# Where the sums over a batch's exponentials stand in the Vector engine's queue, and when the last chunk's exponentials are taken

## The chip, the cores and the metric

The kernel runs on one core of one Trainium2 chip. The time is the device time of one execution in microseconds; a kernel's time is the median of several runs. The kernel before takes 269.26 us (three runs, 268.95 to 269.48).

## The reference

An efficient attention is followed by a layer norm and a two-layer perceptron, for 8 batches of 576 rows, 8 heads of 64 columns (512 columns in all):

```python
q_s = np.exp(q - max(q))                      # over the 64 columns of a head
q_s = q_s / (np.sum(q_s, axis=-1, keepdims=True) + 1e-09)
k_s = exp(k - max(k)) / sum over the rows
kv  = np.einsum('bhsd,bhse->bhde', k_s, v)
x   = np.einsum('bhsd,bhde->bhse', q_s, kv)   # heads side by side: 576 x 512 per batch
xn  = (x - mean) / np.sqrt(var + 1e-06) * g_ln
out = x + np.maximum(xn @ w_ch1, 0.0) @ w_ch2 # 512 -> 2048 -> 512
```

What matters here is the first two lines: for every row and head the exponentials of q are summed, and the reciprocal of the sum scales that head's attention output. The kernel multiplies with the unscaled exponentials first and scales the product afterwards, so the sums are not needed until an attention output is read out of PSUM.

## The kernel before, in words

**Chunks.** A chunk is 512 rows, held as 4 tiles of 128 rows. Chunk c from 0 to 7 is the first 512 rows of batch c; the ninth chunk, `C9` = 8, is the last 64 rows of all eight batches. The chunks' perceptrons run one after the other on TensorE (PE), and everything else is laid beside them: while the perceptron of chunk c runs, the attention of chunk c+1 is computed, and batch c+2 is loaded and its exponentials are taken.

**Stages and positions.** From chunk 2 on the perceptron is written with seven products in place of eight per 2x2 block, and each layer is 112 steps of half a position: the first layer (the first stage, `mm1_fast`, L747) goes from position 0 to 56, the second (the second stage, `mm2_fast`, L677) from 56 to 112. One step is one matmul of 128x128 weights and 256 columns. The order of all engines' instructions is written out by hand: `run` (L830) walks through the matmuls of a chunk and, ahead of each, issues the side work whose position has been reached. Side work at equal positions keeps the order in which it was put on the list. Each engine then works through its own queue in that order and waits there for whatever its next instruction needs.

```python
for weight, go in main:
    while done < len(side) and side[done][0] <= at:
        side[done][1]()
```

**The first stage.** It handles column groups in two halves, groups 0 and 1, then 2 and 3. Each half has seven products with two groups each (`plan`, L788), so each product is 2 positions per group:

```python
(1, "x", True, seed), (5, "b", True, copy_5), (6, "x", False, add_5),
(2, "c", False, relu), (7, "x", False, out_22), (3, "b", False, relu), (4, "x", False, relu)
```

`x`, `b` and `c` are PSUM banks. After product 6 VectorE (DVE) adds `x` and a copy into `b` (`add_5`, L775); product 7 writes on into the same bank `x`, so its first matmul waits until `add_5` of its group has read it. After product 7 DVE makes an output (`out_22`, L778), and after the second group of a half it applies the ReLU to four blocks at once (L783). ScalarE (ACT) makes the copies (L768, L772) and the other ReLUs (L786). `sum_h` (L583) makes the operand sums of the second stage on DVE.

**The second stage.** Products 1, 5, 6, 2, 7, 3 and 4 take 8 positions each. The results are added to the residual by `y_quarter` (L610, eight per chunk), on DVE; the last two read bank `a` after the last product. The PSUM pool has six banks for all of this; the first matmuls on bank `b` of the next chunk wait until `y_quarter` has read the banks that they are put in.

**Attention beside it.** `exp_q` (L193, ACT) writes a batch's exponentials into the tile `eq`, of which there is one buffer; `eq_T` transposes it by a DMA of the SyncE (SP) queue. `reduce_q` (L210, DVE) sums half of the tile over the 64 columns of each head (128x16 sums out of 128x1024 values), twice per chunk, and `recip_q` (L859) takes the reciprocals. `po_mm` multiplies with the key-value product, and `x_fast` (L421, L407, DVE) reads the attention output, scales it by the reciprocals and writes the layer norm's input `xn`. `xn_T` (two DMA transposes on SP, L256) makes `xnT`, and `sum_x` (L248) makes the operand sums `tq` of the next chunk's first stage on GpSimd (POOL); for chunk 7 the second of the four is made on DVE, from the first. `load_batch` writes one element of each input tile on DVE (L1079) ahead of the loads, which SP issues after that.

**The last chunk.** Its rows of q are loaded in chunk 6 (`load_qrem`); `exp_qrem` (L206) takes their exponentials in four pieces on ACT.

Of the kernel before, what the change touches and what calls it, by code (L numbers as in the profile page):

```python
# [20 lines left out]
def kernel(  # L21
# [22 lines left out]
    T = 4  # L44
# [805 lines left out]
    def prep_fast(b):  # L850

        s = [(57, lambda: exp_q(b, 0, 4)), (65, lambda: exp_q(b, 2, 4)), (79, lambda: eq_T(b))]
        s += [(81, lambda: reduce_q(b, 0, 2)), (91, lambda: reduce_q(b, 2, 2))]
        s += [(81, lambda: exp_k(b, 0, 4)), (98, lambda: exp_k(b, 2, 4))]
        s += [(106, lambda: prep_kvrem(b))]
        return s

    def recip_q(c):
        nc.vector.reciprocal(eqs[c][2], eqs[c][1])  # L859

    def attn_fast(c):

        s = [(8, lambda: reduce_q(3, 2, 2))] if c == 3 else []
        s += [(22 if c == 3 else 2, lambda: recip_q(c))]
        s += [(12, lambda: kv_all(c))]
        s += [(40, lambda: start_x(c))]
        for t, (p0, p1) in enumerate(((48, 53), (57, 59), (65, 67), (73, 75))):
            s += spread([lambda t=t, i=i: po_mm(c, t, i) for i in range(NP)], p0, p1)
            s += [(p1, lambda t=t: x_fast(c, t)), ((66, 74, 87, 91)[t], lambda t=t: square_sum(c, t))]
        s += [(61, lambda: xn_T(c, 0, 2)), (78, lambda: xn_T(c, 2, 2)), (95, lambda: rstd_op(c))]  # L870
        s += [((84, 100 if c == C9 - 1 else 88, 92, 101)[i], lambda i=i: sum_x(c, i)) for i in range(4)]
        return s

    def second_side():

        s = [(p, lambda i=i: quarter_w2(i, 1)) for i, p in enumerate((8.5, 13, 44, 46))]
        s += [(8.0, lambda: xn_pT(1, 3, nc.vector))]
        s += [(3, lambda: exp_q(2, 0, 4)), (7, lambda: exp_q(2, 2, 4)), (7.2, lambda: eq_T(2))]
        s += [(42, lambda: square_sum(1, 2)), (67, lambda: square_sum(1, 3)), (71, lambda: rstd_op(1))]
        s += [(7.3, lambda: load_batch(3, (2,), eqTs[2][0:1, T - 1, NP - 1, 0:4])), (31, lambda: load_batch(3, (0,)))]  # L880
        s += [(9 + 2 * j, lambda j=j: cast_v(2, j)) for j in range(2)]
        s += [(7.4, lambda: load_v(3))]
        s += [(93 + j, lambda j=j: cast_v(3, j)) for j in range(2)]
        s += [(15 + 3 * t, lambda t=t: reduce_q(2, t, 2)) for t in (0, 2)]
        s += [(36, lambda: recip_q(2))]
        s += [(18, lambda: exp_k(2, 0, 4)), (22, lambda: exp_k(2, 2, 4)), (26, lambda: prep_kvrem(2))]
        s += [(41, lambda: kv_all(2))]
        s += [(46, lambda: start_x(2))]
        for t, (p0, p1) in enumerate(((52, 54), (57, 59), (62, 65), (70, 74))):
            s += spread([lambda t=t, i=i: po_mm(2, t, i) for i in range(NP)], p0, p1)  # L890
            s += [(p1, lambda t=t: x_fast(2, t)), ((73, 82, 88, 94)[t], lambda t=t: square_sum(2, t))]
        s += [(60, lambda: xn_T(2, 0, 2)), (77, lambda: xn_T(2, 2, 2)), (100, lambda: rstd_op(2))]
        s += [(75, lambda: exp_q(3, 0, 4)), (79, lambda: exp_q(3, 2, 4)), (85, lambda: eq_T(3))]
        s += [(97, lambda: reduce_q(3, 0, 2))]
        s += [(97, lambda: exp_k(3, 0, 4)), (108, lambda: exp_k(3, 2, 4)), (113, lambda: prep_kvrem(3))]
        s += [(p, lambda i=i: sum_w1(i, 1)) for i, p in enumerate((30, 47, 58, 64))]
        s += spread([lambda i=i: sum_x(2, i) for i in range(4)], 95, 108)
        return s

    def attn_rest():  # L900

        s = [(2, lambda: recip_q(C9)), (4, lambda: start_x(C9))]
        for t, (p0, p1, p2) in enumerate(((14, 22, 46), (44, 54, 62), (58, 66, 69), (67, 75, 77))):
            s += [(p0, lambda t=t: [po_mm(C9, t, i) for i in range(NP)])]
            s += [(p1, lambda t=t: x_fast(C9, t)), (p2, lambda t=t: square_sum(C9, t))]
        s += [(61, lambda: xn_T(C9, 0, 2)), (78, lambda: xn_T(C9, 2, 2)), (88, lambda: rstd_op(C9))]
        return s + spread([lambda i=i: sum_x(C9, i) for i in range(4)], 102, 104)
# [179 lines left out]
    with tc.manual_schedule(  # L1087
        engines={mybir.EngineType.PE, mybir.EngineType.DVE, mybir.EngineType.Activation,
                 mybir.EngineType.SP, mybir.EngineType.Pool}
    ):  # L1090
        first_batch()
        load_behind(1, (2, 0))
        load_w2(2)
        load_behind(1, (1,))
        load_w2(3)
        load_behind(2)

        def po_x(c, t):
            for i in range(NP):
                po_mm(c, t, i)  # L1100
            x_fast(c, t)

        run(
            mlp_steps(0),
            [
                (0.5, lambda: xn_pT(0, 1, nc.scalar)),
                (2.5, lambda: (q0_rest(2), x_fast(0, 2))),
                (3.2, lambda: eq_pT(0, 3, nc.scalar)),
                (7, lambda: (q0_rest(3), x_fast(0, 3))),
                (11, lambda: xn_pT(0, 2, nc.scalar)),  # L1110
                (15, lambda: xn_pT(0, 3, nc.scalar)),
                (20, g_columns),
                (24, lambda: square_sum(0, 2)),
                (28, lambda: square_sum(0, 3)),
                (34, lambda: (x_copy(0, 0), square_po(0, 1))),
                (36, lambda: x_copy(0, 1)),
                (37, lambda: nc.vector.tensor_scalar_mul(out=xs[0][3][:, 0, 1:2], in0=xs[0][3][:, 0, 1:2], scalar1=float(DM))),
                (38, lambda: rstd_op(0)),
            ]
            + [(62, lambda: exp_q(1, 0, 4)), (64, lambda: exp_q(1, 2, 4))]  # L1120
            + [(67 + t, lambda t=t: reduce_q(1, t)) for t in range(T)]
            + [((74, 78, 86, 90)[t], lambda t=t: eq_pT(1, t, nc.scalar)) for t in range(T)]
            + [(78, lambda: nc.vector.reciprocal(eqs[1][2], eqs[1][1]))]
            + [(80, lambda: exp_k(1, 0, 4)), (84, lambda: exp_k(1, 2, 4))]
            + [(26 + 4 * i, lambda i=i: scale_w1(i % KO1, i // KO1)) for i in range(2 * KO1)]
            + [(p, lambda i=i: quarter_w2(i, 0)) for i, p in enumerate((55, 58, 60, 62))]
            + [(98.5 + 0.4 * j, lambda j=j: cast_v(1, j)) for j in range(2)]
            + [(p, lambda i=i: sum_w1(i, 0)) for i, p in enumerate((80, 84, 88, 92))]
            + [(100.4, lambda: prep_kvrem(1))]
            + [(100.5, lambda: kv_mm(1, range(T))), (102.0, lambda: (kv_mm(1, range(T, T + 1)), kv_out(1), start_x(1)))]  # L1130
            + [(108.0, lambda: po_x(1, 0)), (110.0, lambda: po_x(1, 1))]
            + [(113.0, lambda: po_x(1, 2)), (114.9, lambda: xn_pT(1, 0, nc.scalar)), (115.9, lambda: square_sum(1, 0))]
            + [(115.9, lambda: po_x(1, 3)), (121.0, lambda: xn_pT(1, 1, nc.scalar)), (122.0, lambda: square_sum(1, 1))]
            + [(128.0, lambda: xn_pT(1, 2, nc.scalar))]

        )
        for c in range(1, B):
            side = []
            if c == 1:
                side += second_side()  # L1140
            else:
                if c + 1 < B:
                    side += attn_fast(c + 1)
                else:
                    side += attn_rest()
                if c + 2 < B:
                    side += [(1, lambda b=c + 2: load_batch(b))]
                    side += [(26, lambda b=c + 2: load_v(b))]
                    side += prep_fast(c + 2)
            if c == B - 2:  # L1150
                side += [(1, load_qrem)]
                side += spread([lambda r=r: exp_qrem(r) for r in range(T)], 34, 50)
                side += [(52, lambda: eq_T(C9))]
                side += [(84 + 4 * t, lambda t=t: reduce_q(C9, t, 2)) for t in (0, 2)]
            sums = [(57, 0)] if c == FAST else [(p, i) for i, p in enumerate((30, 41) if c == B - 1 else (30, 33, 41))]
            run(mlp_steps(c), side + [(at, lambda i=i: sum_h(0, i)) for at, i in sums])
        run(mlp_steps(C9), [(33 + 3 * i, lambda i=i: sum_h(0, i)) for i in range(2)])
# [30 lines left out]
```

## Time and profile before

| | us |
|---|---|
| median of three runs | 269.26 (268.95 to 269.48) |
| profiled execution | 268.44 |
| its span, first to last instruction | 266.6 |
| PE busy | 259.1 (97%) |
| DVE busy | 220.2 (83%) |
| ACT busy | 178.6 (67%) |
| POOL busy | 90.6 (34%) |

The profiled execution is 0.8 us under the median of the runs; 1.8 us of it lie outside the span. Chunk boundaries can be read from the first matmul of a chunk (line L744, `bx<-xnT,w1g`): chunks 2 to 8 begin at 78.77, 105.31, 131.52, 157.73, 183.94, 210.44 and 237.69 us of the span, and the last matmul ends at 262.33. A position of these chunks is 0.218 us (16 matmuls in 1.75 us are 8 positions). Rows of the page and of the timeline give: engine, line, operation, output <- inputs, shape; in brackets the engine's idle time before it and what ended it.

### The profile page before, as it was taken

The page shows a single profiled execution, that of the slowest core. Times are in us where ns is not written, and L with a number is a line of the kernel's source. Part 1 is how long each engine was busy: PE and PEld are TensorE (multiplying, and loading weights), DVE is VectorE, ACT ScalarE, POOL GpSimd, SP SyncE. Part 2 cuts the span into 40 slices and gives each one's busy share as a digit, 9 for nine tenths or more (in the row PEclk, how much of TensorE's full clock was granted, in tenths as well). Part 3 has the DMA queues.
Part 4 walks back from the last instruction along what each step waited for, and adds up shares of the span by engine and source line. Part 5 has one row for each costly group of instructions (what it writes and reads, how often), then busy time and mean ns, then how long its engine had stood idle before and what let it go on. Part 6 is the DMA issues. An engine that isn't in the chain of part 4 may idle for free. (4 is left out here: it accounts for less than half of the span.)

```text
span 266.6 us, 6696 instructions
## 1 busy us (share of the span) xinstructions
PE 259.1 (97%) x2634; PEld 218.4 (82%) x2634; DVE 220.2 (83%) x471; ACT 178.6 (67%) x349; POOL 90.6 (34%) x145
## 2 busy tenths in 40 slices
PE   8999999999999999999999999999999999999993
PEld 5778855775988998899889988998989788888882
DVE  7974995878999899789988988998799968877872
ACT  4767881796966886688668866786686378438400
POOL 6933126213069104930781088109100800030000
PEclk9999999999999999999999999999999999999999
DMA  6999999979966998899589948996935130422014
GB/s 216 220 203 207 325 223 303 278 171 279 176 131 195 303 111 133 246 288 117 92 265 267 127 87 278 257 138 126 261 60 101 42 119 4 79 81 79 2 39 118
DMA packets 82329, 45.00 MB, mean 169 GB/s; under 512 B 58037, under 2 KB 78521, under 8 KB 82298
## 3 DMA queue, kind: packets, MB, share of 16 engines
q0 software_dynamic: 32800, 22.29, 44.9%
q1 hardware_dynamic: 48906, 21.77, 37.6%
q10 hardware_dynamic: 592, 0.52, 0.6%
q8 instruction: 20, 0.33, 0.5%
q14 instruction: 11, 0.09, 0.1%
HBM read 36.70 MB, written 9.44 MB: 173 GB/s over the span
## 5 line engine op out<-in xcount | busy, mean ns | idle before, releaser
L599 PEld LDWEIGHTS <-hs 128*128 128x128 bf16 x512 | 49.5, 98 | 5.7
L744 PEld LDWEIGHTS <-w_q 128*128 128x128 bf16 x448 | 43.0, 98 | 6.8 <-issue 1.0
L248 POOL TENSOR_TENSOR tq<-xnT 128x256 bf16<-128x256 bf16 x24 | 15.6, 665 | 77.2 <-DMA xnT<-xn 63.9
L599 PEld LDWEIGHTS <-hT 128*128 128x128 bf16 x384 | 37.1, 98 | 4.4
L744 PEld LDWEIGHTS <-w1g 128*128 128x128 bf16 x336 | 32.2, 98 | 3.9
L599 PE MATMUL ba<-w_q,hs 128*128 128x256 bf16 x256 | 31.7, 273 | 0.0
L775 DVE TENSOR_TENSOR bb<-bx,s 128x512 f32<-128x512 f32 x28 | 18.3, 695 | 14.1 <-ACT s L772 14.0
L744 PE MATMUL bx<-tq,w_q 128*128 128x256 bf16 x224 | 29.2, 273 | 0.1
L768 ACT COPY bc<-bx 128x512 f32<-128x512 f32 x28 | 15.2, 594 | 16.8 <-PE bx L744 16.8
L421 DVE SCALAR_TENSOR_TENSOR x<-po,rq 128x512 bf16<-128x512 f32 x34 | 23.3, 686 | 2.2 <-PE po L370 2.0
L395 ACT ACTIVATE scrap<-x,mv 128x512 bf16<-128x512 bf16 x32 | 23.0, 720 | 1.7 <-DVE x L421 1.3
L616 POOL DMA_DIRECT2D out_dram<-ot x28 | 15.4, 558 | 24.1 <-DVE ot L610 24.0
L786 ACT ACTIVATE hT<-bc 128x512 bf16<-128x512 f32 x28 | 15.5, 598 | 11.7 <-PE bc L744 11.7
L583 DVE TENSOR_TENSOR hs<-hT 128x1024 bf16<-128x1024 bf16 x32 | 21.7, 685 | 1.3 <-ACT hT L786 1.2
L370 PE MATMUL po<-kv_sb,eqT 128*128 128x128 bf16 x128 | 21.2, 219 | 0.0
L210 DVE TENSOR_REDUCE zq<-eq 128x16 f32<-128x1024 bf16 (+1 forms) x20 | 20.6, 1048 | 0.5 <-ACT eq L193 0.5
L778 DVE TENSOR_TENSOR hT<-bx,s 128x512 bf16<-128x512 f32 x28 | 18.0, 686 | 3.2 <-PE bx L744 3.2
L786 ACT ACTIVATE hT<-bb 128x512 bf16<-128x512 f32 x28 | 15.3, 600 | 8.1 <-PE bb L744 8.1
L624 ACT COPY s<-ba 128x512 f32<-128x512 f32 x15 | 8.7, 579 | 13.4 <-PE ba L599 8.7
L599 PE MATMUL ba<-w_sb,hT 128*128 128x256 bf16 x128 | 16.7, 273 | 0.0
L599 PE MATMUL bb<-w_q,hs 128*128 128x256 bf16 x128 | 16.6, 273 | 0.0
L772 ACT COPY s<-bb 128x512 f32<-128x512 f32 x28 | 15.8, 620 | 0.7 <-PE bb L744 0.7
(152 smaller groups left out, 555.1 us busy)
## 6 DMA issues: line engine op xcount, KB each, us to landing
out_dram<-ot POOLq DMA_DIRECT2D x32, 256.0 KB, 6.2
qt<-in_q_dram SPq DMA_DIRECT2D x5, 1024.0 KB, 6.8
kt<-in_k_dram SPq DMA_DIRECT2D x5, 1024.0 KB, 13.4
w_sb<-in_moe_w_ch_dram POOLq DMA_DIRECT2D x4, 512.0 KB, 16.5
qt<-in_q_dram POOLq DMA_DIRECT2D x2, 1024.0 KB, 14.6
kt<-in_k_dram POOLq DMA_DIRECT2D x2, 1024.0 KB, 15.2
vm<-in_v_dram POOLq DMA_DIRECT2D x16, 128.0 KB, 13.0
w_raw<-in_moe_w_ch_dram POOLq DMA_DIRECT2D x3, 512.0 KB, 12.3
```

The lines of the kernel that those rows point to most:

```text
L210: nc.vector.reduce_sum(eqs[c][1][:, ts], eqs[c][0][:, ts], axis=AX.X)
L248: eng.tensor_tensor(out=dst[:, t], in0=x[:, t], in1=y[:, t], op=ALU.subtract)
L370: nc.tensor.matmul(pobox["p"][:, i * P : i * P + P], eqTs[c][:, t, i, :], kv_sb[:, c, i, :], start=True, stop=True,)
L395: nc.scalar.activation(scrap, x[:, t], AF.Square, bias=mv[:, t, 0:1], scale=-float(DM), accum_out=mv[:, t, 1:2],)
L421: nc.vector.scalar_tensor_tensor(x[:, t].rearrange("p (h d) -> p h d", h=H), in0=pobox[c, t].rearrange("p (h d) -> p h d", h=H), scalar=1. ...
L583: nc.vector.tensor_tensor(out=dst, in0=x, in1=y, op=op)
L599: nc.tensor.matmul(hbox[bank][:, t], lhsT, rhs, start=first and (own or t == 0) and k == 0, stop=k == KH - 1, skip_group_check=True)
L744: nc.tensor.matmul(dst[:, q], lhsT, rhs, start=first and q == 0 and ko == 0, stop=ko == 1, skip_group_check=True)
L772: nc.scalar.copy(at[g, "s"], at[g, "b"])
L775: nc.vector.tensor_tensor(out=at[g, "b"], in0=at[g, "x"], in1=at[g, "s"], op=ALU.add)
L778: nc.vector.tensor_tensor(out=h_out(g, 1, 1), in0=at[g, "x"], in1=at[g, "s"], op=ALU.add)
L786: nc.scalar.activation(h_out(g, odd, half), at[g, name], AF.Relu)
```

## The change

Three things are moved; no instruction is added or taken away, and no shape is changed.

- The two sums of a batch (`reduce_q`) leave the second stage of the chunk in which its exponentials are taken (positions 81 and 91; for batch 3, position 97 of chunk 1 and position 8 of chunk 2) and go into the first stage of the next chunk, to positions 1 and 27. The reciprocal goes from position 2 (batch 3: 22) to 28.
- The same for the ninth chunk: its sums go from positions 84 and 88 of chunk 6 to 1 and 27 of chunk 7, the reciprocal from 2 to 28, and the first `x_fast` of it from 22 to 31.
- In chunk 6 the ninth chunk's exponentials go from positions 34 to 50 (first stage) to 58 to 80 (second stage), and their transpose from 52 to 84.

```diff
     def prep_fast(b):
         s = [(57, lambda: exp_q(b, 0, 4)), (65, lambda: exp_q(b, 2, 4)), (79, lambda: eq_T(b))]
-        s += [(81, lambda: reduce_q(b, 0, 2)), (91, lambda: reduce_q(b, 2, 2))]
         s += [(81, lambda: exp_k(b, 0, 4)), (98, lambda: exp_k(b, 2, 4))]
...
     def attn_fast(c):
-        s = [(8, lambda: reduce_q(3, 2, 2))] if c == 3 else []
-        s += [(22 if c == 3 else 2, lambda: recip_q(c))]
+        s = [(1, lambda: reduce_q(c, 0, 2)), (27, lambda: reduce_q(c, 2, 2)), (28, lambda: recip_q(c))]
         s += [(12, lambda: kv_all(c))]
...
     def second_side():
-        s += [(97, lambda: reduce_q(3, 0, 2))]
...
     def attn_rest():
-        s = [(2, lambda: recip_q(C9)), (4, lambda: start_x(C9))]
-        for t, (p0, p1, p2) in enumerate(((14, 22, 46), (44, 54, 62), (58, 66, 69), (67, 75, 77))):
+        s = [(1, lambda: reduce_q(C9, 0, 2)), (27, lambda: reduce_q(C9, 2, 2)), (28, lambda: recip_q(C9)), (4, lambda: start_x(C9))]
+        for t, (p0, p1, p2) in enumerate(((14, 31, 46), (44, 54, 62), (58, 66, 69), (67, 75, 77))):
...
             if c == B - 2:
                 side += [(1, load_qrem)]
-                side += spread([lambda r=r: exp_qrem(r) for r in range(T)], 34, 50)
-                side += [(52, lambda: eq_T(C9))]
-                side += [(84 + 4 * t, lambda t=t: reduce_q(C9, t, 2)) for t in (0, 2)]
+                side += spread([lambda r=r: exp_qrem(r) for r in range(T)], 58, 80)
+                side += [(84, lambda: eq_T(C9))]
```

On DVE the order around the moved instructions becomes: last `y_quarter`, first sum, `load_batch`'s two writes, `add_5` of groups 0 and 1; and in the middle of the first stage: ReLU (L783), second sum, reciprocal, the two `sum_h`, `add_5` of groups 2 and 3. PE's and POOL's queues keep their order. On SP the ninth chunk's transpose goes behind chunk 7's two `xn_T`.

## The prediction

> **What bounds the kernel now.** First the waits of PE, then the busy time chunk by chunk, then the timelines around what was left.
>
> ```profile
> PE bb L744 <- DVE ot L610: 0.7, 2, 0.5
> PE bb L744 <- DVE kt L1079: 0.2, 1, 0.2
> ```
>
> ```profile
> 78.77:105.31 26.54, 26.37 (x282) 23.34 (x280) 24.54 (x52) 19.72 (x38) 10.66 (x17) 1.00 1.15 187
> 131.52:157.73 26.21, 26.21 (x282) 23.45 (x280) 22.87 (x49) 19.63 (x38) 11.79 (x18) 1.00 1.03 189
> ...
> 183.94:210.44 26.50, 26.37 (x282) 23.43 (x280) 22.92 (x46) 17.49 (x37) 6.59 (x12) 1.00 0.51 119
> 210.44:237.69 27.25, 26.59 (x258) 22.51 (x256) 22.32 (x53) 15.69 (x33) 3.68 (x7) 1.00 0.21 60
> ```
>
> The columns are the chunk's length, then busy PE, weight load, DVE, ACT, POOL, the granted clock, and DMA. Chunks 3, 4 and 5 take 26.21 us each with PE busy throughout: nothing is left to gain there, however much DVE is relieved. Chunk 2 is 0.33 us longer and chunk 6 0.29; chunk 7 has another mix of matmuls and is read from its timeline. The stalls, in PE's timeline at the starts of chunks 2 and 7 and in the middle of chunk 6:
>
> ```profile
> 80.42 0.60 PE L744 MATMUL bb<-tq,w_q 128*128 128x256 bf16 x4 [0.17 <-DVE kt L1079]
> ```
>
> ```profile
> 194.41 1.33 PE L744 MATMUL bx<-tq,w_q 128*128 128x256 bf16 x8
> ```
>
> ```profile
> 211.97 0.61 PE L744 MATMUL bb<-tq,w_q 128*128 128x256 bf16 x4 [0.49 <-DVE ot L610]
> 212.75 0.60 PE L744 MATMUL bb<-tq,w_q 128*128 128x256 bf16 x4 [0.17 <-DVE ot L610]
> ```
>
> A matmul is issued every 0.109 us, so 4 should be followed after 0.44 us and 8 after 0.87. Chunk 2: the first four on `bb` begin at 79.64 and the next at 80.42 in place of 80.08, 0.33 lost (the `kt` named there stands in DVE's count beside the last `ot`, which ends at 80.36). Chunk 6: eight take 1.33 where others take 1.04, 0.30 lost. Chunk 7 begins at 210.44 with eight: 211.97 in place of 211.31, 0.66, and 212.75 in place of 212.41, 0.33. All waits from chunk 2 on make 1.62 us: the most that this change could win.
>
> **The change part by part.** Twelve sums at 1.21 us (1.13 from start to start) and six reciprocals at 0.34 (L859) keep their number; only places differ.
>
> *End of chunk 1.* DVE before:
>
> ```profile
> 75.42 1.21 DVE L210 TENSOR_REDUCE zq<-eq 128x16 f32<-128x1024 bf16 x1
> ...
> 79.49 0.87 DVE L610 SCALAR_TENSOR_TENSOR ot<-ba,rstd,x 128x256 f32<-128x256 f32 x2
> ```
>
> Without the sum at 75.42 all that follows comes 1.13 us earlier, until it waits for PE: bank `a` is complete 0.2 us after the chunk's end, so the last `ot` ends at 79.85 in place of 80.36. PE wants it at 80.08. The 0.33 us goes, and the bank then has 0.2 to spare, as in chunks 3 to 5. -0.33.
>
> *First sum at position 1, chunks 2 to 7.* It stands between the last `ot` and `add_5`. DVE idles there now (chunk 4):
>
> ```profile
> 132.53 0.34 DVE L859 RECIPROCAL rq<-zq 128x32 f32<-128x32 f32 x1
> 133.96 1.30 DVE L775 TENSOR_TENSOR bb<-bx,s 128x512 f32<-128x512 f32 x2 [1.09 <-ACT s L772]
> ```
>
> From 132.53 a sum ends at 133.74, before 133.96: nothing, with 0.2 us of cover; in chunk 7 (212.62 + 1.13 against 213.88) 0.1. If the cover were gone, `add_5` and after it product 7 would be late by what is missing; the bound is the 0.1 or 0.2 that a longer sum could take, and the twelve sums vary by 0.01. Queued behind it are `load_batch`'s writes, and behind those SP's loads of qt, kt and ktr, which start 1.1 us later in chunks 3 to 5 and 0.6 in chunk 2. They land about 6.8 and 13.4 us after issue (DMA rows), some 6 and 5 us before the exponentials read them: nothing. The DMA queue behind them is fullest in chunk 2, where `tq` can start only at 103.51; its second sum is needed at 106.7 and is done at 106.06, so even 0.6 us is covered, barely.
>
> *Second sum and reciprocal at 27 and 28.* Chunk 4 now:
>
> ```profile
> 137.84 0.47 DVE L783 TENSOR_SCALAR hT<-hT 128x1024 bf16<-128x1024 bf16 x1
> 138.51 0.69 DVE L583 TENSOR_TENSOR hs<-hT 128x1024 bf16<-128x1024 bf16 x1 [0.20 <-ACT hT L786]
> 139.24 0.69 DVE L583 TENSOR_TENSOR hs<-hs,hT 128x1024 bf16<-128x1024 bf16 x1
> 140.97 1.30 DVE L775 TENSOR_TENSOR bb<-bx,s 128x512 f32<-128x512 f32 x2 [1.04 <-ACT s L772]
> ```
>
> Idle are 0.20 + 1.04; needed are 1.24 (sum, and 0.035 until its result is read) and 0.33. From the start of L783, with its usual 0.43: +0.34 sum, +1.24 reciprocal, +0.33 and +0.72 the `sum_h`, +0.60 `add_5`: 3.24, where it now starts 3.13 after. `add_5` of group 3 ends at +4.54, and 0.05 later (the 195.09 to 195.14 of chunk 6's stall) PE may go on; PE wants it at +4.59 (chunk 3: 111.63 to 116.22). So the slack of 0.11 is used up to the last hundredth: 0.00 with L783 at 0.43, 0.04 with 0.47. In chunk 5 it took longer, beside POOL's issues of the v loads:
>
> ```profile
> 164.05 0.73 DVE L783 TENSOR_SCALAR hT<-hT 128x1024 bf16<-128x1024 bf16 x1
> ```
>
> There the same sum gives 0.30. Of the fourteen L783 twelve take 0.43; of the four that lie beside v loads two do, one 0.47, one 0.73. I take the 0.43 of most for three chunks and chunk 4's 0.47: +0.04; the bounds are 0 and 4 x 0.30 = 1.2. In chunk 7 `x_fast` (1.0) stands there too: `add_5` 0.39 later, but four pairs of 64-row matmuls (0.34) delay PE as well: nothing, up to 0.1.
>
> Why a long L783 occurs is weighed against the Trainium skill, "SBUF — State Buffer", section "Who interferes with whom": a `tensor_scalar` in a two-port mode and GpSimd take one shared pair of SBUF ports as an exclusive lock, and the later one waits fully. By that, any of chunks 2 to 5 can be hit, not chunk 5 alone; the trace agrees in one or two of four. By the rows the term is +0.04, by the rule up to +1.2, and the sum would be the slower rival's below.
>
> *Chunk 6's exponentials.* ACT at 193.20, 194.20 and on has four of 0.68 us between its copies, and `add_5` of group 3 waits 0.30 for the copy behind the first. Moved, they no longer stand there; the sum and reciprocal at 27 and 28 now do, at the 0.00 above. -0.30. In the second stage ACT has room: chunks 2 to 5 carry 4.6 us of exponentials there (two of 1.06, two more, one of 0.41) and are not late; here it is 2.8. The transpose lands at about 209 in place of 201; its reader is at 214.6.
>
> *Start of chunk 7.* DVE and POOL at the end of chunk 6:
>
> ```profile
> 207.17 1.21 DVE L210 TENSOR_REDUCE zq<-eq 128x16 f32<-128x1024 bf16 x1
> 208.33 1.42 DVE L248 TENSOR_TENSOR tq<-xnT,tq 128x256 bf16<-128x256 bf16 x2
> ```
>
> ```profile
> 207.63 2.64 POOL L248 TENSOR_TENSOR tq<-xnT 128x256 bf16<-128x256 bf16 x4 [19.91 <-DMA xnT<-xn]
> ```
>
> Two sums leave, and yet I book nothing. DVE's `tq` reads POOL's first result, complete 0.67 after 207.63, at 208.30: just when the sum let go. Behind `tq` come one addition and six `ot`, without a gap, and the last of them releases the bank at 212.70. What is late next is `xnT`, whose DMA took 3.9 us here. In chunks 3 and 5 it took 3.3, with an `eqT` queued behind as there will be now, and 3.0 in chunk 7. So the bounds are -0.86 (3.0 and DVE free) and +0.3 (the transpose behind it delays it further). Value: 0, from the 3.9 of this place.
>
> Sum: -0.33 + 0.04 - 0.30 + 0 = -0.59. The profiled execution (268.44, 266.6 of span and 1.8 around it) would take 267.85. It lies 0.82 under the median of the runs; against that median: 268.67.
>
> **The rivals.**
>
> *Chunk 7's start is won too.* For it: the `xnT` of chunks 3, 5 and 7 took 3.3, 3.3 and 3.0, and DVE is now free to use an early one. Against: the `xnT` of chunk 6 keeps its place. With 3.3 it is 0.6 more, 268.07; at most 267.8.
>
> *One chunk meets a long L783 as chunk 5 does now.* 0.30 back: -0.29, 268.97, the same within what can be told.
>
> *Slower: the middle of the first stage is overfull.* Second sum and reciprocal leave DVE no idle time before `add_5`, so every lengthening of L783 goes to PE, and all of chunks 2 to 5 meet it: 4 x 0.30 = 1.2 against 0.63 won: +0.57, 269.83. (It is this that the rule of the Trainium skill, "SBUF — State Buffer", "Who interferes with whom", would bring about.) It decides from three chunks on. For it: slack of 0.00, and the change of timing on POOL; against: chunks 2 and 3 at 0.43 beside the same v loads.
>
> *`eqT` behind `xnT` delays chunk 7:* +0.3, 268.97.
>
> **How the numbers follow.** 0.2% is 0.54 us, about what a measurement of this kernel can tell from no change. Forecast (nothing met, or a few hundredths): 0.30, two thirds of it beyond 0.54. Chunk 7 won: 0.32, nearly all faster. One long L783: 0.18, same. Overfull: 0.12, slower. `eqT` late: 0.08, half same, half slower with a long L783 besides. Faster 0.20 + 0.30 = 0.50; same 0.10 + 0.02 + 0.18 + 0.04 = 0.34; slower 0.16. The range goes from 267.9 (chunk 7 won almost whole) to 269.6 (two or three long L783 and a late `eqT`).
>
> **What would show it.** Chunks 2 and 6 at 26.21 to 26.25 us; no wait of PE `bb` on `ot` at chunk 2; a sum right before each first `add_5`, which still shows a short wait for ACT; second `add_5` with no idle time before it, 3.24 us after L783's start. Chunk 7 at 27.25 says that `xnT` holds it, at 26.4 that the sums did. I am wrong if chunks 3 to 5 grow past 26.3: then `bx<-tq,w_q` of their second half takes more than 1.04.

## The result, and the profile after

| | before | after |
|---|---|---|
| median of 11 runs each, us | 269.26 (268.95 to 269.75) | 268.32 (267.28 to 268.97) |
| ratio | | 0.9963, 95% interval 0.995 to 0.9977 |
| profiled execution, us | 268.44 | 268.63 |
| its span, us | 266.6 | 266.8 |
| from the start of chunk 2 to the last matmul's start, us | 183.27 | 182.67 |

The changed kernel is faster, by 0.4%; the forecast was 268.67. A second measurement, with its own runs of the kernel before on the same chip, gave 268.54 against 269.30, a ratio of 0.9976 (0.9967 to 0.9985).

The two profiled executions seem to say the opposite, 268.63 against 268.44. The reason stands ahead of everything that the change touches. These are the busy times by stretch of the kernel before and then of the changed kernel; the columns are length, PE, weight load, DVE, ACT, POOL, granted clock, DMA share, GB/s:

```profile
0.00:78.77 78.77, 76.55 (x755) 56.96 (x756) 62.91 (x146) 55.86 (x106) 30.24 (x53) 1.00 1.09 231
```

```profile
0.00:79.51 79.51, 77.18 (x751) 58.03 (x755) 62.50 (x146) 55.96 (x106) 30.29 (x53) 0.98 1.08 229
```

Chunk 2 begins 0.74 us later, at a mean clock of 0.98: for 3.4 us near the start the clock was granted at half. Some traces of either kind have such a stretch and some have none (3.4 us in the kernel before with eight more writes, none in the changed one with the late v loads, both below), so the traces are compared from the start of chunk 2 on, where the clock is 1.00 in all of them.

From there on, chunk by chunk, the changed kernel:

```profile
79.51:105.85 26.34, 26.34 (x283) 23.43 (x280) 23.21 (x49) 19.63 (x38) 10.15 (x17) 1.00 1.18 188
105.85:132.30 26.45, 26.45 (x283) 23.42 (x280) 23.32 (x49) 19.63 (x38) 14.01 (x23) 1.00 1.05 187
132.30:158.55 26.25, 26.25 (x282) 23.45 (x280) 23.12 (x49) 19.62 (x38) 11.84 (x18) 1.00 1.10 189
158.55:185.02 26.47, 26.47 (x283) 23.42 (x281) 23.34 (x49) 19.63 (x38) 12.44 (x20) 1.00 1.06 188
185.02:211.23 26.21, 26.21 (x283) 23.46 (x281) 23.49 (x48) 17.60 (x37) 7.25 (x13) 1.00 0.53 121
211.23:237.84 26.61, 26.44 (x259) 22.51 (x257) 23.85 (x54) 15.61 (x33) 3.04 (x6) 1.00 0.22 61
```

Against the kernel before (26.54, 26.21, 26.21, 26.21, 26.50, 27.25) chunk 2 is 0.20 shorter, chunks 3, 4 and 5 are 0.24, 0.04 and 0.26 longer, chunk 6 is 0.29 shorter and chunk 7 0.64. The sum is -0.60, and the forecast's sum was -0.59. Two of its terms were badly off, and the two errors cancelled: that the totals agree is luck.

The waits of PE that are left from chunk 2 on, by the view of its waits, come down to one:

```profile
PE bb L744 <- DVE ot L610: 0.2, 1, 0.2
```

The view names only a wait that follows an idle engine. The new stalls of chunks 2 to 5 are not in it, since a matmul's modelled end covers them; they are found in PE's timeline, where eight matmuls take more than 1.04 us. The rows are of chunk 2's start, chunk 3's middle, chunk 6's middle and chunk 7's start:

```profile
80.38 1.04 PE L744 MATMUL bb<-tq,w_q 128*128 128x256 bf16 x8
...
116.40 1.20 PE L744 MATMUL bx<-tq,w_q 128*128 128x256 bf16 x8
...
195.49 1.04 PE L744 MATMUL bx<-tq,w_q 128*128 128x256 bf16 x8
...
212.11 0.61 PE L744 MATMUL bb<-tq,w_q 128*128 128x256 bf16 x4
212.89 0.60 PE L744 MATMUL bb<-tq,w_q 128*128 128x256 bf16 x4 [0.17 <-DVE ot L610]
```

The first and third are the two won stalls: 0.33 and 0.30 are gone. The second is new. At chunk 7 the first four on `bb` are not held up any more (0.66 before); the 0.33 ahead of the second four is still there.

What holds chunk 3's middle is read from DVE's timeline there:

```profile
112.17 0.79 DVE L783 TENSOR_SCALAR hT<-hT 128x1024 bf16<-128x1024 bf16 x1
112.88 1.20 DVE L210 TENSOR_REDUCE zq<-eq 128x16 f32<-128x1024 bf16 x1
114.11 0.35 DVE L858 RECIPROCAL rq<-zq 128x32 f32<-128x32 f32 x1
114.38 0.63 DVE L583 TENSOR_TENSOR hs<-hT 128x1024 bf16<-128x1024 bf16 x1
115.05 0.69 DVE L583 TENSOR_TENSOR hs<-hs,hT 128x1024 bf16<-128x1024 bf16 x1
115.66 1.29 DVE L775 TENSOR_TENSOR bb<-bx,s 128x512 f32<-128x512 f32 x2
```

There is no idle time in brackets anywhere: sum, reciprocal, two operand sums and `add_5` follow L783 back to back, and L783 took 0.79 us instead of 0.43. From its start to `add_5` are 3.49 us. In chunks 2 to 5 the four L783 that stand there took 0.68, 0.79, 0.60 and 0.81, and PE's stall at product 7 was 0.13, 0.25, 0.05 and 0.27 over the two column groups (by the chunks' lengths 0.13, 0.24, 0.04 and 0.26).

Chunk 7's start, DVE and then POOL:

```profile
206.19 0.88 DVE L610 SCALAR_TENSOR_TENSOR ot<-bc,rstd,x 128x256 f32<-128x256 f32 x2
208.46 1.43 DVE L248 TENSOR_TENSOR tq<-xnT,tq 128x256 bf16<-128x256 bf16 x2 [1.40 <-POOL tq L248]
209.81 0.69 DVE L627 TENSOR_TENSOR bb<-bb,s 128x512 f32<-128x512 f32 x1
```

```profile
207.77 2.65 POOL L248 TENSOR_TENSOR tq<-xnT 128x256 bf16<-128x256 bf16 x4 [18.96 <-DMA xnT<-xn]
```

DVE now idles for 1.40 us ahead of `tq`, and `tq` begins 2.77 us before chunk 7 (211.23) where it began 2.11 before (208.33, 210.44). These 0.66 us are the 0.64 won. It begins earlier because POOL does, and POOL because `xnT` landed 3.25 us after its issue and not 3.90.

### The profile page after: what moved, and what is told of

It is laid out like the page before. It is cut to its first block, busy times and chain, and to the rows that moved or that the text cites. A ratio compares the mean times of both kernels' runs of the same rounds, so it can differ in the third digit from the quotient of the medians.

```text
span 266.8 us, 6690 instructions
## 1 busy us (share of the span) xinstructions
PE 260.0 (97%) x2631; PEld 219.5 (82%) x2634; DVE 221.5 (83%) x471; ACT 178.6 (67%) x349; POOL 90.7 (34%) x145
## 5 line engine op out<-in xcount | busy, mean ns | idle before, releaser
L744 PEld LDWEIGHTS <-w_q 128*128 128x128 bf16 x448 | 43.0, 98 | 6.1 <-issue 0.7
L744 PEld LDWEIGHTS <-w1g 128*128 128x128 bf16 x336 | 32.2, 98 | 3.9
L744 PE MATMUL bx<-tq,w_q 128*128 128x256 bf16 x224 | 29.5, 272 | 0.0
L552 PE MATMUL pc<-w_sb,hT 128*128 128x512 bf16 x61 | 15.6, 379 | 0.2
```

The source lines that it names most:

```text
L552: nc.tensor.matmul(hbox["pc", t], hbox["h"][:, ko, t, :], w2_sb[:, ko, :], start=(ko == 0), stop=(ko == KO2 - 1),)
L744: nc.tensor.matmul(dst[:, q], lhsT, rhs, start=first and q == 0 and ko == 0, stop=ko == 1, skip_group_check=True)
```

## The experiments

Three questions were open: whether the middle of the first stage is lost to a long L783 or to the load of DVE in itself; what lengthens L783; and why `xnT` came earlier though nothing of its own was moved. Lengths of chunks 2 to 7 of each kernel's trace, the sum from the start of chunk 2 to the last matmul's start, and the landing of the second `xnT` of chunk 6 after its issue:

| kernel | 2 | 3 | 4 | 5 | 6 | 7 | sum | `xnT` |
|---|---|---|---|---|---|---|---|---|
| before | 26.54 | 26.21 | 26.21 | 26.21 | 26.50 | 27.25 | 183.27 | 3.90 |
| before, run again | 26.54 | 26.21 | 26.21 | 26.21 | 26.50 | 27.25 | 183.27 | 3.90 |
| after | 26.34 | 26.45 | 26.25 | 26.47 | 26.21 | 26.61 | 182.67 | 3.25 |
| after, run again | 26.34 | 26.21 | 26.23 | 26.32 | 26.21 | 26.62 | 182.26 | 3.26 |
| reciprocal late | 26.21 | 26.21 | 26.21 | 26.21 | 26.21 | 26.66 | 182.05 | 3.23 |
| v loads after L783 | 26.21 | 26.21 | 26.21 | 26.21 | 26.21 | 26.60 | 182.00 | 3.24 |
| ninth chunk's sums back | 26.54 | 26.27 | 26.46 | 26.21 | 26.21 | 26.29 | 182.32 | 3.29 |
| exponentials back | 26.34 | 26.21 | 26.37 | 26.42 | 26.49 | 26.39 | 182.56 | 3.03 |
| batches 4 to 7 back | 26.34 | 26.21 | 26.21 | 26.21 | 26.21 | 26.64 | 182.16 | 3.27 |
| best of the changes | 26.21 | 26.21 | 26.21 | 26.21 | 26.21 | 26.26 | 181.65 | 3.31 |
| late v loads, POOL sums | 26.21 | 26.21 | 26.21 | 26.21 | 26.21 | 26.26 | 181.65 | 4.10 |
| before, 8 more writes | 26.55 | 26.21 | 26.21 | 26.21 | 26.49 | 27.04 | 183.06 | 3.04 |
| after, 7 more writes | 26.35 | 26.21 | 26.28 | 26.21 | 26.21 | 27.45 | 183.06 | 4.09 |

### The kernel before, once more

No edit.

> The kernel before, profiled once more, to see which of its readings repeat. The stalls at the starts of chunk 2 (0.33 us) and in chunk 6 (0.30) should be there again: both follow from the order of the queues. Chunk 7's start: if xnT's late landing (3.9 us) comes from the instruction fetch that fell on its end, and this fetch follows from DVE's place in its program, xnT lands in 3.9 us again, the stall is 0.99 and chunk 7 takes 27.2. If it was chance, xnT lands in 3.0 to 3.3 and, by the run with the ninth chunk's sums back, chunk 7 takes about 26.3.

269.06 us, 183.27 from chunk 2 on: chunk for chunk the same as the first trace, as expected. The changed kernel repeats less well (182.67 and 182.26), and the whole difference lies in the stalls of chunks 2 to 5. One thing did differ between the two traces of the kernel before: of the L783 beside the v loads three were long (0.71, 0.73, 0.50) where the first trace had one of 0.73 and one of 0.47. With idle time of DVE behind them, they cost nothing.

### The reciprocal late

The sums stay in the first stage, and only the reciprocal leaves its crowded middle.

```diff
-        s = [(1, lambda: reduce_q(c, 0, 2)), (27, lambda: reduce_q(c, 2, 2)), (28, lambda: recip_q(c))]
+        s = [(1, lambda: reduce_q(c, 0, 2)), (27, lambda: reduce_q(c, 2, 2)), (49, lambda: recip_q(c))]
```

> The changed kernel with one move: the reciprocal of chunks 3 to 7 from position 28 to 49, behind the ReLU of the second half. Theory (the middle of the first stage is overfull): the second sum alone fits into DVE's 1.24 us of idle time even with a long ReLU, so the four stalls of PE ahead of product 7 in chunks 2 to 5 (0.14, 0.25, 0.05 and 0.27 us in the changed kernel's profile) go, and each of these chunks takes 26.21 us; 0.7 us in all. The ReLU at L783 stays as long as it is (0.6 to 0.8 us in three or four of them). Rival (the ReLU beside the v loads is what costs, whatever stands behind it): the stalls stay within 0.1 us. Second rival (the reciprocal is late for x_fast instead): chunks 2 to 5 lose as much in their second stage or at the next start.

All stalls in the middle are gone, 26.21 in chunks 2 to 6, though three of the four L783 were as long as in the changed kernel. DVE's timeline of chunk 4:

```profile
139.37 0.70 DVE L783 TENSOR_SCALAR hT<-hT 128x1024 bf16<-128x1024 bf16 x1
139.99 1.20 DVE L210 TENSOR_REDUCE zq<-eq 128x16 f32<-128x1024 bf16 x1
141.12 0.67 DVE L583 TENSOR_TENSOR hs<-hT 128x1024 bf16<-128x1024 bf16 x1
141.82 0.69 DVE L583 TENSOR_TENSOR hs<-hs,hT 128x1024 bf16<-128x1024 bf16 x1
142.49 1.30 DVE L775 TENSOR_TENSOR bb<-bx,s 128x512 f32<-128x512 f32 x2
```

From L783 to `add_5` are 3.12 us, against 3.49. PE's product 7 is not late at 3.12. So a long L783 costs nothing even with the sum behind it; it costs PE something only where the 0.27 us of the reciprocal stand there too. The single execution took 269.18 us (before: 269.55); its chunk 2 begins at 80.63, 1.12 later than in the changed kernel, so only its chunks are compared.

### The v loads after L783

POOL issues the v loads at position 26, right beside L783. Here a small copy on POOL that reads L783's output is put ahead of them, so that no v load is issued while L783 runs; the reciprocal stays at 28.

```diff
+                    side += [(26, lambda: nc.gpsimd.tensor_copy(out=gate, in_=hbox["h"][:, 1, 2, 0:4]))]
```

> The changed kernel with a four-column copy on POOL ahead of the v loads, which reads an output of the first half's ReLU: POOL issues the v loads only after that ReLU. Theory (a v load's issue on POOL and the ReLU on DVE exclude each other): the ReLU of the first half takes 0.43 us in chunks 2 to 5, in place of 0.68, 0.79, 0.60 and 0.81, and the stalls ahead of product 7 fall to 0.05 or less each. Rival (the ReLU is long for another reason): it stays at 0.6 to 0.8 and the stalls stay. Beside that the v loads run some 2 us later, which may delay xnT in chunk 2 and cost up to 2 us at the start of chunk 3; that is read apart.

The instructions of L783 in this kernel, and in the changed one (minimum, median and maximum of fourteen, in ns):

```profile
L783 DVE TENSOR_SCALAR hT<-hT x14: 426/427/428, 84.7 to 247.6; 128x1024 bf16<-128x1024 bf16 x14
```

```profile
L783 DVE TENSOR_SCALAR hT<-hT x14: 426/428/806, 85.8 to 249.4; 128x1024 bf16<-128x1024 bf16 x14
```

Without an issue beside it no L783 is long, chunks 2 to 6 take 26.21 each, and the later v loads delay nothing. The one execution took 266.82 us.

That it is the issue and not the transfer can be seen in the changed kernel itself: while its four long L783 ran, no packet was moving on queue 0 (`software_dynamic`), where POOL's transfers go. How long L783 becomes follows from where among the issues it starts. POOL has four of them in a row, one about every 0.9 us; those of chunk 3, beside the L783 that starts at 112.17:

```profile
111.79 3.57 POOL L147 DMA_DIRECT2D vm<-in_v_dram  x4
```

The eleven traces in which the v loads are not held back have 44 such L783:

| L783 starts after an issue's start by, us | times | L783 takes, us |
|---|---|---|
| 0.01 to 0.21 | 5 | 0.43; it is the issue that takes longer, up to 1.12 in place of 0.93 |
| 0.30 to 0.71 | 33 | 0.88 down to 0.47; it ends 1.17 to 1.18 after the issue's start |
| 0.74 to 0.86 | 6 | 0.43 |

So L783 waits until about 0.75 us of the issue are over (an estimate: 1.18 less its own 0.43), unless it came first by enough to make the issue wait. What differs between executions is this offset. In chunk 2 it hardly differs: in the three traces with the sums where they were, L783 starts 0.02 us ahead of an issue and takes 0.43, and in all eight with the sums moved 0.36 to 0.57 ahead of one and takes 0.68 to 0.88. There the change itself moved L783 into the bad place, by a way that these traces do not show.

The Trainium skill, "SBUF — State Buffer", section "Who interferes with whom", describes such a lock between a `tensor_scalar` in a two-port mode and GpSimd. The trace agrees as to who disturbs whom and that the earlier one makes the other wait; but L783 went on 0.75 us into an issue of 0.93 and not at its end, and the loss was at most 0.45 us, less than the 0.9 of one issue (POOL's row has four in 3.57).

### The ninth chunk's sums back

Everything as changed, but the ninth chunk's sums go back to the end of chunk 6.

```diff
-        s = [(1, lambda: reduce_q(C9, 0, 2)), (27, lambda: reduce_q(C9, 2, 2)), (28, lambda: recip_q(C9)), (4, lambda: start_x(C9))]
+        s = [(2, lambda: recip_q(C9)), (4, lambda: start_x(C9))]
...
+                side += [(84 + 4 * t, lambda t=t: reduce_q(C9, t, 2)) for t in (0, 2)]
```

> The changed kernel with the ninth chunk's two sums, its reciprocal and its first x_fast where they were before (84 and 88 in chunk 6, 2 and 22 in chunk 7); its exponentials stay in the second stage. Theory (the sums on DVE hold back tq and the bank reads at the end of chunk 6): chunk 7 takes 27.2 us as before, 0.64 more than in the changed kernel. Rival (it was only the earlier landing of xnT, 3.3 us in place of 3.9): chunk 7 stays at 26.6 as long as xnT lands in 3.3 us.

Chunk 7 took 26.29, shorter than with the sums moved away: that the sums hold `tq` back is not enough as a reason. DVE and POOL here:

```profile
207.77 1.21 DVE L210 TENSOR_REDUCE zq<-eq 128x16 f32<-128x1024 bf16 x1
208.90 0.48 DVE L248 TENSOR_TENSOR tq<-xnT,tq 128x256 bf16<-128x256 bf16 x2
```

```profile
207.62 2.91 POOL L248 TENSOR_TENSOR tq<-xnT 128x256 bf16<-128x256 bf16 x4 [18.59 <-DMA xnT<-xn]
```

`tq` on DVE begins no earlier than in the kernel before (2.14 us ahead of chunk 7, 2.11 there), but the pair takes 0.48 us instead of 1.42. One by one: 0.28 each here, 0.75 each there. Both of its inputs lie in SBUF, and POOL's own sums run beside it. Here DVE's first began at 208.90, within 0.02 of POOL's third, and it was POOL that became longer (1.03 against 0.71). In the kernel before DVE's two begin 0.06 and 0.11 us after an operation of POOL, and it is DVE that becomes longer. The pair is 0.94 us shorter and chunk 7 0.96: that the difference is one of phase is read from this one trace, and no run shifts the phase alone.

### The exponentials back

```diff
-                side += spread([lambda r=r: exp_qrem(r) for r in range(T)], 58, 80)
-                side += [(84, lambda: eq_T(C9))]
+                side += spread([lambda r=r: exp_qrem(r) for r in range(T)], 34, 50)
+                side += [(52, lambda: eq_T(C9))]
```

> The changed kernel with the ninth chunk's exponentials and their transpose where they were before (34 to 50, and 52); the sums stay moved. Theory: ACT's copies in the second half of chunk 6's first stage are 0.3 us late again, add_5 of group 3 waits for them and chunk 6 takes 26.5 us in place of 26.21. Chunk 7: if the transpose behind xnT was what made xnT land in 3.3 us in place of 3.9, it takes 3.9 again and chunk 7 26.6 + 0.6 = 27.2; if that was chance, or an effect of the sums, it stays at 26.6.

Chunk 6 returns to 26.49, with a stall of 0.29 at product 7, that of the kernel before: the move of the exponentials is worth 0.29 by itself. Without the `eqT` behind it `xnT` took 3.03 and chunk 7 was 26.39 rather than 26.61, below both values expected, so the transpose that moved behind `xnT` costs up to 0.22. The time was 268.73 us, in one execution.

### Batches 4 to 7 back

Only batch 3 (chunk 2) and the ninth chunk keep the new places.

```diff
+        s += [(81, lambda: reduce_q(b, 0, 2)), (91, lambda: reduce_q(b, 2, 2))]
...
-        s = [(1, lambda: reduce_q(c, 0, 2)), (27, lambda: reduce_q(c, 2, 2)), (28, lambda: recip_q(c))]
+        s = [(1, lambda: reduce_q(3, 0, 2)), (27, lambda: reduce_q(3, 2, 2))] if c == 3 else []
+        s += [(28 if c == 3 else 2, lambda: recip_q(c))]
```

> The changed kernel with the sums and reciprocals of batches 4 to 7 where they were before (81 and 91 of the chunk before, 2), so that only batch 3's and the ninth chunk's are moved. Theory (in chunks 3 to 5 there was nothing to win at the end of the chunk, and the middle of the first stage is overfull): chunks 3, 4 and 5 take 26.21 us again and lose the 0.05 to 0.25 each of the changed kernel; chunk 2 keeps its stall in the middle (0.1 to 0.3) and no stall at its start; from chunk 2 to the end 0.5 us less than the changed kernel. Rival (the relief at the chunks' ends also helps where no wait is to be seen): chunks 3 to 5 take longer than 26.21.

Chunks 3 to 6 take 26.21, with L783 of up to 0.57 beside the loads, and chunk 2 keeps its 0.13. The time was 267.91 us, 0.9951 of the kernel before (0.993 to 0.9972). From chunk 2 on it is 0.51 less than the first trace of the changed kernel and 0.10 less than the second. The four batches gained nothing by the move and lost what the long L783 costs.

### The best of the changes, in two ways

The first takes the late reciprocal, and the second the late v loads; both give all four operand sums of chunk 7 to POOL, so that DVE's `tq` is no longer there to be held.

```diff
-        eng = nc.vector if c == C9 or (c == C9 - 1 and i == 1) else nc.gpsimd
+        eng = nc.vector if c == C9 else nc.gpsimd
...
-        s += [((84, 100 if c == C9 - 1 else 88, 92, 101)[i], lambda i=i: sum_x(c, i)) for i in range(4)]
+        s += [((84, 88, 92, 101)[i], lambda i=i: sum_x(c, i)) for i in range(4)]
```

> The changed kernel with the reciprocal at position 49 and, for chunk 7, all four sums of x on POOL, at the positions of the other chunks. Theory: chunks 2 to 6 take 26.21 us each; at the end of chunk 6 DVE no longer runs its pair for tq beside POOL's (0.75 us each in place of 0.28 alone), so the bank reads wait for PE alone and chunk 7 takes 26.27, 0.34 less than in the changed kernel; 1.0 us less than the changed kernel from chunk 2 on, and 1.6 less than the kernel before. Rival (POOL's longer chain is late for chunk 7's products): a stall of PE on tq in chunk 7 in place of the one on the bank.

> The same for chunk 7, and in place of the later reciprocal the copy on POOL that holds the v loads back until the first half's ReLU is done. Theory: ReLU 0.43 us in every chunk, chunks 2 to 6 at 26.21, chunk 7 at 26.27, so the same time as with the reciprocal at 49, to 0.1 us. If the order of sum and reciprocal alone is at its limit, as reckoned from the rows, a few hundredths of a stall per chunk may be left here and not there.

In neither does PE have a stall left at the places named so far. The first kernel's chunks 6 and 7:

```profile
184.46:210.67 26.21, 26.21 (x283) 23.45 (x281) 23.00 (x47) 17.60 (x37) 7.17 (x13) 1.00 0.53 121
210.67:236.92 26.25, 26.25 (x258) 22.62 (x256) 23.22 (x52) 15.52 (x33) 4.29 (x8) 1.00 0.22 62
```

181.65 us each, 1.62 less than before, which is the whole of the 1.62 that the forecast read from PE's waits as the most that could be won. On the clock: 267.83 us, 0.9943 (0.9923 to 0.9963), and 267.51 us, 0.9937 (0.992 to 0.9955). Both beat the kernel before, and their intervals lie below the changed kernel's second one (0.9967 to 0.9985), though they overlap its first (0.995 to 0.9977). The second has the late `xnT` of 4.10 and the same chunk 7: with the four sums on POOL, 0.8 us of `xnT` cost nothing.

### The late xnT: before with eight more writes, after with seven

What is in common to the kernels with an `xnT` of 3.9 to 4.1 is a packet on queue 14, a fetch of instructions of 8 KB, between its issue and its landing. In the kernel before it starts 4.3 us ahead of chunk 7, in the changed one 1.0. DVE's queue has 452 instructions, waits included, ahead of the second of its two `tq` in the one and 445 in the other (450 and 443 ahead of the first); over the kernels above the fetch comes the earlier, the larger this number is (1.6 us ahead of chunk 7 at 447 and 449, 11.0 at 455). So it was shifted by one-element writes to an unused tile at the start of the kernel, on DVE:

```diff
+        for i in range(8):
+            nc.vector.memset(pad[:, i : i + 1], 0.0)
```

in the kernel before, and the same with 7, which makes 452 again, in the changed one.

> The kernel before, with eight one-element writes on the Vector engine at the very start (a tile nobody reads) and nothing else. They cost some 0.5 us at most, before chunk 2. Theory A, chunk 7's first transposed input is late in the kernel before because an 8 KB fetch of instructions falls into the same 4 us: eight more instructions of the Vector engine ahead shift that fetch to an earlier time, the second xnT of chunk 6 lands in 3.0 to 3.3 us in place of 3.9, and chunk 7 takes 26.3 to 26.7 in place of 27.25, with the sums still at the end of chunk 6. Time 0.5 to 0.9 us less than the kernel before. Theory B, the transposed input is late for the traffic around it (the order of the loads, the missing transpose behind it): 3.9 and 27.25 stay.

> The changed kernel with seven one-element writes on the Vector engine at the very start, so that as many of its instructions stand ahead of chunk 7's first tq as in the kernel before (452). Theory A (the fetch): the fetch goes back to some 4.3 us ahead of chunk 7, the second xnT of chunk 6 takes 3.9 again, and chunk 7 goes from 26.6 to about 27.2: 0.5 to 0.65 us longer from chunk 2 to the end than the changed kernel, and so little or nothing faster than the kernel before. Theory B: 3.25 and 26.6 stay, and the time is that of the changed kernel.

> The changed kernel unaltered, on the same chip as the two with more writes. Both theories: 268.3 to 268.5, 182.67 us from chunk 2 to the end, chunk 7 at 26.6 with the second xnT of chunk 6 at 3.25; it is the ground for the comparison of the other two, and a second measurement of the gain (0.9963 of the kernel before by the first).

The traffic between issue and landing of this `xnT`, in the kernel before, in the changed one, and in the changed one with seven writes (queue, packets, MB, share; then the transpose's time to landing):

```profile
q1 hardware_dynamic: 1317, 0.32, 41.7%
q8 instruction: 1, 0.02, 1.6%
q14 instruction: 1, 0.01, 0.5%
...
xnT<-xn SPq DMA_TRANSPOSE x1, 3.9
```

```profile
q1 hardware_dynamic: 2165, 0.54, 79.4%
...
xnT<-xn SPq DMA_TRANSPOSE x1, 3.2
```

```profile
q14 instruction: 1, 0.01, 0.5%
...
xnT<-xn SPq DMA_TRANSPOSE x1, 4.1
```

The kernel before has a second fetch there, of 16 KB on queue 8. It is not the cause: it starts 3.6 us after the issue, and when this kernel was run again there was none between issue and landing, and `xnT` took 3.90 all the same. (The two kernels with more writes have one line more near the top, so L744 is L745 there.) Seven writes early in the kernel bring back the fetch (4.2 us ahead of chunk 7), the late landing and the stall, in PE's timeline at chunk 7 of that kernel:

```profile
211.16 1.04 PE L745 MATMUL bx<-xnT,w1g 128*128 128x256 bf16 x8
212.89 0.61 PE L745 MATMUL bb<-tq,w_q 128*128 128x256 bf16 x4 [0.70 <-DVE ot L611]
```

Chunk 7 is 27.45 against 26.62 of the changed kernel on the same chip, 0.83 longer and more than the 0.5 to 0.65 expected, and the times are 269.38 and 268.54. Against the kernel before the ratio is 1.0003 (0.9989 to 1.0016): the gain is gone. The changed kernel itself kept its chunk 7 and its `xnT`, as both theories had it, but came to 182.26 from chunk 2 on in place of the expected 182.67, since its L783 were shorter this time. That the fetch is what makes `xnT` late is shown in both directions, since eight writes in the kernel before move the fetch to 11.7 us ahead, and there `xnT` takes 3.04.

The time expected of the latter, 0.5 to 0.9 less, did not come: chunk 7 is 27.04 in place of the expected 26.3 to 26.7, 0.21 less than before, and the ratio is 1.0 (0.9983 to 1.0016). With the sums still at the end of chunk 6, DVE is not free for the early `xnT` (its timeline):

```profile
207.53 1.21 DVE L211 TENSOR_REDUCE zq<-eq 128x16 f32<-128x1024 bf16 x1
208.66 1.24 DVE L249 TENSOR_TENSOR tq<-xnT,tq 128x256 bf16<-128x256 bf16 x2
```

POOL's first sum began at 207.15 and was complete at about 207.8, but DVE's `tq` follows the sum at 208.66, 2.15 us ahead of chunk 7, as before. So at chunk 7's start two things bound at the same time. Sums there and a late `xnT`: 27.25. Sums away with a late `xnT`: 27.45, 0.20 more, with the `eqT` now behind it. Early `xnT` with the sums there: 27.04. Both: 26.61. How DVE's pair of `tq` falls beside POOL's comes on top: early `xnT` with the sums there was 26.29 in the kernel with the ninth chunk's sums back, where the pair took 0.48 and not 1.24.

## Why the prediction was right in its total and wrong in two terms

**Start of chunk 2 (-0.33): right.** The wait of PE for `ot` is gone, and eight on `bb` take 1.04. The last `ot` ends 1.08 us after the chunk's start, as reckoned (79.85 less 78.77).

**First sums at position 1 (0): right.** No kernel shows a stall of PE at the first half's product 7, nor one from the later loads of q and k.

**Second sum and reciprocal at 27 and 28 (+0.04, bounds 0 to 1.2): mis-sized, +0.67.** (0.70 by the stalls.) The failed step is "I take the 0.43 of most for three chunks and chunk 4's 0.47". The one execution at hand showed two of four L783 lengthened, and only one much. Run again, the same kernel has three, and with eight more writes one; wherever sums were moved and the v loads not held back, it is three or four of four. The step counted the lengths of one execution. They follow from where L783 starts among POOL's issues; the change shifted that in chunk 2, and it differs by execution in chunks 3 to 5. The mechanism is that of the rival "Slower: the middle of the first stage is overfull", which was given 0.12 and met all of chunks 2 to 5; the forecast's own sign of being wrong, chunks 3 to 5 past 26.3, came in chunks 3 and 5 (26.45 and 26.47). What kept it from costing 1.2 is a slack that the sum put at 0.00 and that is 0.11: from L783's start to `add_5` the chain is 3.49 with an L783 of 0.79, which is 3.13 with one of 0.43, and the forecast had 3.24. The reciprocal occupies 0.27 there, not 0.33, and the first `sum_h` 0.67. With 0.11 to 0.12 of slack each stall follows: 0.68 gives 0.13, 0.79 gives 0.25, 0.60 gives 0.05, 0.81 gives 0.27, and the 0.88 in chunk 2 of the kernel with the ninth chunk's sums back gives 0.33. Since the lengths differ by execution, the loss does too: 0.67 in the first trace of the changed kernel, 0.26 in the second (0.13, 0.02 and 0.11). In chunk 7 `add_5` came 0.27 later in place of 0.39, and cost nothing, as forecast.

**Chunk 6's exponentials (-0.30): right**, 0.29 by undoing them alone.

**Start of chunk 7 (0, bounds -0.86 to +0.3): mis-sized, -0.64.** The failed step is "Value: 0, from the 3.9 of this place". The reasoning behind it held: with an `xnT` as late as that the moved sums win nothing, 27.45 with the fetch put back, within its bound of +0.3. But 3.9 was no property of the place. It was a fetch of DVE's instructions, which happened to fall into that transpose, and taking seven instructions out of the queue ahead moved it away. The rival "Chunk 7's start is won too", with its 0.6 from an `xnT` of 3.3, is what happened. The `eqT` behind `xnT` costs something: 3.03 without and 3.25 with it where no fetch is near, and chunk 7 26.39 and 26.61.

**The sum** is -0.59 forecast and -0.60 measured, with an error of +0.63 in one term and of -0.64 in the other. That they cancel is luck: they have nothing to do with each other, and the second trace of the changed kernel gives -1.01. The cases named the two mechanisms; their chances treated them as exclusive, though each concerns its own stretch of the kernel and both occurred in one execution. The medians' gains, 0.94 in the first measurement and 0.76 in the second, lie between those of the two traces of the changed kernel, 0.60 and 1.01, which differ by the length of L783.

## What to carry to other kernels

A gap that is filled to the last hundredth has to be priced with the longest duration of each instruction in it that another engine can lengthen, and one execution does not show how often that occurs: here it was two of four in one and four of four in another. Look at where such an instruction starts against the other engine's, since a few tenths of a microsecond decide, and a change can shift them. Work that is not needed soon goes to a place that has idle time (the reciprocal at 49 was free). When one DMA of a kind is slower than its like elsewhere, look in its window for an instruction fetch before the number is booked as a property of the place: adding or removing a few instructions moves it.

## What the runs showed of the hardware

- **An instruction fetch can delay a small transfer by much more than its own length.** The 8 KB packet took 0.31 to 0.39 us, and the `xnT` around it landed 0.79 to 0.86 us later than in the kernel that is its like (3.90 against 3.04, 4.09 against 3.26, 4.10 against 3.31). Seven one-element writes 200 us earlier cost 0.8 us in this way. The Trainium skill, "Runtime: NRT & Kernel Launch", section "Instruction fetch mechanics", calls the cost of such a refill "mostly hidden" and gives blocks of 16 KiB. In these traces queue 8 has packets of 16 KB and queue 14 of 8 KB, and the cost of this one came by way of another transfer. Why 0.31 us become 0.8 is open. In the kernel before the transpose's own packets ended 2.87 us after its issue, with the fetch moved away 2.60; so the larger part of the 0.86 came between the last packet and the landing.
- **Two sums in SBUF at once.** A 128x256 `tensor_tensor` on DVE with both inputs in SBUF took 0.28 us where it began within 0.02 us of POOL's, and 0.75 where POOL's had run for 0.06 or 0.11; POOL's took 0.66 or 0.71, and 1.03 in the first of these cases, which one trace has.
- **A `tensor_scalar` beside a DMA issue of POOL** took 0.47 to 0.88 us instead of 0.43 where it started 0.30 to 0.71 us after an issue's start (33 of 44), and ended 1.17 to 1.18 us after that start. Where it started at most 0.21 after, the issue became longer instead, up to 1.12 for 0.93. It took 0.43 in all fourteen once the issues were held back.
